# A gated mix of attention and feed-forward: the Q scratch holds whole 51-row tiles, and the maximum over partitions moves from GpSimd to TensorE and VectorE

## The chip, the cores and the metric

The kernel runs on one core of a Trainium2 chip. The metric is the device time of one execution in microseconds (us), as the median of several runs. Beside the timed runs one execution was recorded by the hardware profiler; all rows below come from that one.

## The reference

A token block x (2048 x 512) goes through two branches that a gate mixes:

```python
g = sigmoid((x * gate_w).sum(-1, keepdims=True))
q = (x @ wq).reshape(B, S, H, Dh).transpose(0, 2, 1, 3)    # 32 heads of 16
k, v = x @ wk, x @ wv                                      # one head, shared
p = softmax(einsum("bhqd,bkd->bhqk", q, k) * Dh ** -0.5)
a = einsum("bhqk,bkd->bhqd", p, v)....reshape(B, S, H * Dh) @ wo
b = (gelu(x @ w_gate) * (x @ w_up)) @ w_down               # width 1376
return g * a + (1 - g) * b
```

## The kernel before

**Precision.** Every operand is split into a rounded high part and the remainder (`split`, L105 and L106), and a product is made of three TensorE passes. For the scores this is packed into one matmul: the 51 rows (`QK`) of a Q tile are 32 rows of Q (high part and remainder, 16 each), 16 rows of the high part once more (together 48, `KR`), and three rows of a shift. The tile `kp` holds the matching rows of K, and in its last row the number that the shift subtracts before the exponential. A Q tile `Q[u]` has two such groups of 51 partitions (from partition 0 and from partition 64), and two heads in each group, so a unit `u` covers four heads and 512 tokens. There are 32 units (4 token groups of 8 units).

**Prologue.** The loop over token groups runs in the order 1, 2, 3, 0. For each group TensorE projects K and V (`pk`) and then Q in four blocks of 128 columns (`pq`, through the PSUM buffers of `ps_s`, three of them). `post_q` (L176 to L182) takes a block out of PSUM: ScalarE copies the high part into `q2`, VectorE takes the absolute maximum into `qmx` and subtracts for the remainder, and SyncE stores `q2` into the DRAM scratch `scr[tg, b]`, 32 rows for 8 heads. `q2` has three buffers, so the copy of a block waits until the store three blocks earlier has landed. GpSimd writes the shift rows of all heads into a second scratch `shs` (L149), with 0, 0 and 1.

In the last group (token group 0) more work is laid in: a weight fetch `fetch_w(2)` on SyncE ahead of the group's stores, `split_w(0)` and `split_w(1)` on VectorE and GpSimd, `post_v`, and behind the third block `load_q(0)` and `load_q(1)`, which read the first two Q tiles back. `load_q` issues six DMAs for a unit: two of 32 rows, two of 16 rows that read the high part a second time (`load_qk`, L235 and L236), and two of 3 rows out of `shs` (L245). SyncE's queue works in the order of the program, and a DMA that has to wait holds up all that stand behind it.

**Bound and branch.** Then the largest |q| times the largest |k| bounds all scores. VectorE reduces `qmx` and `kmx` to one number per partition (L272, L273), GpSimd reduces over the partitions (`partition_all_reduce` into `mma`, L274), VectorE makes the product `cb`, the `flag` whether it is too large, and `row`, the shift, which goes into the last row of both groups of `kp` by two DMAs (L425). `fill(2)` (L426) issues the gate and the up projection of the first feed-forward chunk. Every engine loads the flag into a register and branches (L431, L432): if the flag is set, a long block computes exact maxima. With these inputs it is skipped, and each engine jumps over it.

**Main loop.** For each unit and each of 16 key blocks TensorE makes scores (`s`, L487), ScalarE their exponential (`p`, L490), TensorE the product with V (`acc`, L557), interleaved by the list `ORDER` with pieces of the feed-forward branch (`fill`): the gate `g`, the up projection `u` and the down projection `dn` of a chunk, by `chain_mm` (L299). The first scores come behind the gate of the second chunk. Q tiles have two buffers; unit `u + 1` is loaded at the third key block of unit `u`, on the same SyncE queue as the weight chunks (`st`, L196).

Of the kernel before, what the change touches and what calls it, by code (L numbers as in the profile page):

```python
# [19 lines left out]
P = 128  # L20
S = 2048
D = 512
H = 32
DH = 16
F = 1376
TG = 512
NTG = S // TG
# [3 lines left out]
NB = 4  # L31
KR = 48
QK = 51
# [12 lines left out]
def mix_kernel(ctx, tc, xT, wq, wkv, wo, wf, out):  # L46
    nc = tc.nc
    cp = ctx.enter_context(tc.tile_pool(name="cp", bufs=1))
    dr = ctx.enter_context(tc.tile_pool(name="dr", bufs=1, space=DRAM))
    ps_s = ctx.enter_context(tc.tile_pool(name="ps_s", bufs=3, space=PSUM))  # L50
# [1 line left out]
    ps_f = ctx.enter_context(tc.tile_pool(name="ps_f", bufs=1, space=PSUM))  # L52
    ctx.enter_context(tc.manual_schedule())

    scr = dr.tile([NTG, NB, 32, 8, TG], F32, name="scr")
    shs = dr.tile([NTG, 3, H, TG], F32, name="shs")

    kp = cp.tile([P, S], F32R, name="kp")
    v1 = cp.tile([P, NKC, 32], F32, name="v1")
# [6 lines left out]
    qmx = cp.tile([P, NTG * NB], F32, name="qmx")  # L66
    kmx = cp.tile([P, NTG], F32, name="kmx")
    mm2 = cp.tile([P, 2], F32, name="mm2")
    mma = cp.tile([P, 2], F32, name="mma")
    cb = cp.tile([P, 1], F32, name="cb")  # L70
    sh = cp.tile([P, 1], F32, name="sh")
    flag = cp.tile([P, 1], I32, name="flag")
    woh = cp.tile([P, NB, D], F32R, name="woh")
    wol = cp.tile([P, NB, D], F32R, name="wol")

# [34 lines left out]
    ident = cp.tile([P, P], F32, name="ident")  # L110
# [34 lines left out]
    zz = woh[0:H]  # L145
    nc.gpsimd.memset(zz.bitcast(F32), 0.0)
    nc.gpsimd.memset(zz[:, 2].bitcast(F32), 1.0)
    for g in range(NTG):
        nc.gpsimd.dma_start(shs[g].rearrange("r h q -> h r q"), zz[:, 0:3].bitcast(F32))  # L149

    def passes(ps, lh, ll, rh, rl, n, first=True, last=True):
        seq = [(i, a, b) for i in range(n) for a, b in ((lh, rh), (ll, rh), (lh, rl))]
        for q, (i, a, b) in enumerate(seq):
            nc.tensor.matmul(ps, a(i), b(i), start=(first and q == 0), stop=(last and q == len(seq) - 1),
                             skip_group_check=True)

    def post_k(tg, pk):
        sl = slice(tg * TG, (tg + 1) * TG)
        for r in (0, 64):
            nc.scalar.copy(kp[r : r + KR, sl], pk[0:KR])  # L160
        nc.scalar.copy(vt[32 * tg : 32 * tg + 32], pk[64:96])
        nc.vector.tensor_reduce(kmx[0:KR, tg : tg + 1], pk[0:KR], axis=AX, op=ALU.max, apply_absolute_value=True)
        for r in (32, 96):
            nc.vector.tensor_sub(kp[r : r + 16, sl], pk[32:48], kp[r : r + 16, sl])
# [8 lines left out]
            nc.vector.tensor_copy(v2[:, i::4, 16:32], t[:, :, 0:16])  # L173
            nc.vector.tensor_copy(zt[:, i::4], t[:, :, 16:17].rearrange("p g r -> p (g r)"))

    def post_q(tg, b, pq):  # L176
        q2 = p2.tile([P, 2, TG], F32R, tag="q2", name=f"q2{tg}_{b}", bufs=3)
        i = tg * NB + b
        nc.scalar.copy(q2[:, 0], pq)
        nc.vector.tensor_reduce(qmx[:, i : i + 1], pq, axis=AX, op=ALU.max, apply_absolute_value=True)  # L180
        nc.vector.tensor_sub(q2[:, 1], pq, q2[:, 0])
        nc.sync.dma_start(scr[tg, b].rearrange("(t d) h q -> (d h) t q", t=2), q2.bitcast(F32))  # L182

    chunks = [(tg, f) for tg in range(NTG) for f in range(NF)]
    W = {}
# [7 lines left out]
    def fetch_w(n):  # L193
        if n < len(chunks):
            stage[n] = cp.tile([P, 3, D], F32, tag="st", name=f"st{n}", bufs=2)
            nc.sync.dma_start(stage[n], wf[chunks[n][1]].rearrange("p (t d) -> p t d", t=3))  # L196
# [30 lines left out]

    Q = {}

    def load_qk(t, u):  # L230
        g, ub = divmod(u, 8)
        b, a = divmod(ub, 2)
        for j in range(2):
            hs = slice(4 * a + j, 4 * a + 4, 2)
            nc.sync.dma_start(t[64 * j : 64 * j + 32].bitcast(F32), scr[g, b, 0:32, hs])  # L235
            nc.sync.dma_start(t[64 * j + 32 : 64 * j + KR].bitcast(F32), scr[g, b, 0:16, hs])  # L236

    def load_q(u, shift=True, data=True):
        g, ub = divmod(u, 8)
        if data:  # L240
            Q[u] = cp.tile([P, 2, TG], F32R, tag="Q", name=f"Q{u}", bufs=2)
            load_qk(Q[u], u)
        if shift:
            for j in range(2):
                nc.sync.dma_start(Q[u][64 * j + KR : 64 * j + QK].bitcast(F32), shs[g, :, 4 * ub + j : 4 * ub + 4 : 2])  # L245

    fetch_w(0)
    fetch_w(1)
    for ti, tg in enumerate(order):
        if ti == NTG - 1:  # L250
            fetch_w(2)
        xh, xl = xs[tg]
        pk = ps_a.tile([P, TG], F32, tag="pa", name=f"pk{tg}")
        passes(pk, lambda c: wkh[:, c], lambda c: wkl[:, c], lambda c: xh[:, c], lambda c: xl[:, c], NC)
        post_k(tg, pk)
        for b in range(NB):
            pq = ps_s.tile([P, 2 * TG], F32, tag="s", name=f"pq{tg}_{b}")[:, 0:TG]
            bs = slice(b * P, (b + 1) * P)
            passes(pq, lambda c: wqh[:, c, bs], lambda c: wql[:, c, bs], lambda c: xh[:, c], lambda c: xl[:, c], NC)
            if ti + 1 < NTG:  # L260
                split_x(order[ti + 1], b)
            post_q(tg, b, pq)
            if ti == NTG - 1 and b == 0:
                split_w(0)
            if ti == NTG - 1 and b == 1:
                post_v()
            if ti == NTG - 1 and b == 2:
                load_q(0)
                load_q(1)
                split_w(1)  # L270

    nc.vector.tensor_reduce(mm2[:, 0:1], qmx, axis=AX, op=ALU.max)  # L272
    nc.vector.tensor_reduce(mm2[:, 1:2], kmx, axis=AX, op=ALU.max)  # L273
    nc.gpsimd.partition_all_reduce(mma, mm2, P, bass_isa.ReduceOp.max)  # L274
    nc.scalar.activation(gt, zt, AF.Tanh, bias=0.0, scale=0.5)
    nc.vector.tensor_scalar(gc, gt, -0.5, 0.5, op0=ALU.mult, op1=ALU.add)
    nc.vector.tensor_scalar(gt, gt, 0.5, 0.5, op0=ALU.mult, op1=ALU.add)
# [131 lines left out]
    def fill(k=1):  # L409
        for _ in range(k):  # L410
            next(filler, None)
# [4 lines left out]
                for fn in later.pop(s):  # L416
                    fn()

    nc.vector.tensor_mul(cb, mma[:, 0:1], mma[:, 1:2])
    nc.vector.tensor_scalar(flag, cb, BOUND / DH, None, op0=ALU.is_gt)  # L420
    nc.vector.tensor_scalar(sh, cb, -1.01 * DH, None, op0=ALU.mult)
    row = zz[0:1].rearrange("p a b -> p (a b)")
    nc.vector.tensor_scalar(row, row, 0.0, sh[0:1], op0=ALU.mult, op1=ALU.add)
    for r in (QK - 1, 64 + QK - 1):
        nc.sync.dma_start(kp[r : r + 1].bitcast(F32), row.bitcast(F32))  # L425
    fill(2)  # L426
    pro.close()
    mp = ctx.enter_context(tc.tile_pool(name="mp", bufs=1))
    base = now[0] + 1
# [2 lines left out]
    with tc.If(v > 0):  # L432
        with tc.tile_pool(name="gp", bufs=1) as gp:
            zr = gp.tile([1, S], F32, name="zr")
            nc.vector.memset(zr, 0.0)
            for r in (QK - 1, 64 + QK - 1):
                nc.sync.dma_start(kp[r : r + 1].bitcast(F32), zr)
            for g in range(NTG):
                mx = gp.tile([P, 4, H, 2], F32, tag="mx", name=f"mx{g}")
                for ub in range(8):  # L440
                    t = gp.tile([P, 2, TG], F32R, tag="gq", name=f"gq{g}_{ub}", bufs=2)
                    load_qk(t, 8 * g + ub)
# [22 lines left out]
                nc.sync.dma_start(shs[g].rearrange("r h q -> h r q"), nb.bitcast(F32))  # L465
            load_q(0, data=False)
            load_q(1, data=False)


    m2 = ctx.enter_context(tc.tile_pool(name="m2", bufs=1))  # L470
# [115 lines left out]
    g = NTG - 1  # L586
# [50 lines left out]
```

## Time and profile before

| | us |
|---|---|
| median of 3 runs | 1305.08 |
| lowest and highest | 1304.79, 1305.23 |
| the profiled execution | 1305.77 |
| its span, from the first to the last instruction | 1304.0 |
| TensorE busy (matmul) | 1282.3 |
| ScalarE busy | 1023.1 |
| VectorE busy | 545.2 |
| GpSimd busy | 208.8 |

The profile counts an engine as busy while it executes; matmuls are pipelined, and their ends are modelled. L12 is line 12 of the kernel file. A row of the timeline gives the start and the duration in us, engine, line, operation, output from inputs, the count, and in brackets the idle time before it and what ended that. SPq is SyncE's queue of DMA issues; a name with q at its end (PEldq, DVEq) is the sequencer of that engine. The DMA share is the mean busy share of the 16 DMA engines.

### The profile page before, as it was taken

The numbers are of one execution on the slowest core, as the hardware profiler recorded it, in microseconds if no ns is written. First come the engines' busy times: TensorE is split into PE (matmuls) and PEld (weight loads), VectorE is DVE, ScalarE is ACT, GpSimd is POOL, SyncE is SP. The second block draws the span as 40 slices with busy tenths as digits, with TensorE's granted clock in tenths as the row PEclk, the third lists the DMA queues.
The fourth block names the chain that finished last, engine by engine and source line by source line (L and its number), as shares of the span: only waits on it lengthen the run. The fifth ranks groups of instructions, "written<-read, shape, count | busy, mean of one in ns | idle before, by whom it ended". The sixth has DMA issues, their size and how long they took to land.

```text
span 1304.0 us, 20303 instructions
## 1 busy us (share of the span) xinstructions
PE 1282.3 (98%) x8178; PEld 648.0 (50%) x8178; DVE 545.2 (42%) x829; ACT 1023.1 (78%) x1118; POOL 208.8 (16%) x173
## 2 busy tenths in 40 slices
PE   9969999999999999999999999999999999999998
PEld 6844445444454444445444455454445444445444
DVE  6753352624443162633435144252526134344334
ACT  5338888888888788888888878888887788888884
POOL 3122121202120021121212012021122011202010
PEclk9979999999999999999999999999999999999999
DMA  8441011111110211111111021110211211011100
GB/s 307 143 142 52 30 35 62 37 62 49 59 38 1 70 62 38 62 37 47 41 46 38 30 78 38 62 38 2 78 54 38 70 62 38 11 52 38 38 1 33
DMA packets 25204, 72.43 MB, mean 56 GB/s; under 512 B 3888, under 2 KB 3920, under 8 KB 25104
## 3 DMA queue, kind: packets, MB, share of 16 engines
q1 hardware_dynamic: 24704, 70.02, 16.0%
q8 instruction: 66, 1.08, 0.3%
q0 software_dynamic: 256, 0.79, 0.1%
q10 hardware_dynamic: 144, 0.26, 0.1%
q14 instruction: 34, 0.28, 0.1%
HBM read 57.67 MB, written 13.37 MB: 54 GB/s over the span
## 4 chain that ended last, share of the span: by engine, by line
PE 90%; ACT 2%; issue 1%; DVE 0%; ACTq 0%; DVEq 0%
PE acc L557 36%; PE s L487 23%; PE g L299 10%; PE u L299 10%; PE dn L299 8%; PE wo L299 3%; ACT p L490 2%; PE wos L299 1%; DVE acc L310 0%; PE wof L299 0%; DVE sq L362 0%; DVE sq L355 0%; DVE gs L384 0%; ACT sq L359 0%; ACTq L490 0%
## 5 line engine op out<-in xcount | busy, mean ns | idle before, releaser
L490 ACT ACTIVATE p<-s 128x1024 f32<-128x1024 f32 x1024 | 972.7, 1028 | 213.3 <-PE s L487 207.9
L557 PE MATMUL acc<-p,v 128*32 128x512 f32 x4096 | 479.2, 597 | 0.0
L487 PE MATMUL s<-Q,kp 51*128 51x512 f32 x2048 | 337.2, 429 | 4.5 <-ACT p L490 4.5
L487 PEld LDWEIGHTS s<-Q,kp 51*128 51x128 f32 x2048 | 165.0, 184 | 243.8 <-issue 160.2
L106 POOL TENSOR_TENSOR gl<-st,gh 128x512 fp32r<-128x512 f32 x88 | 122.8, 1415 | 994.8 <-DVE gh L105 783.1
L557 PEld LDWEIGHTS acc<-p,v 128*32 128x32 f32 x4096 | 113.5, 109 | 259.4 <-issue 253.1
L338 DVE SCALAR_TENSOR_TENSOR acc<-dn,gc,acc 128x512 f32<-128x512 f32 x48 | 35.7, 745 | 203.6 <-PE dn L299 203.6
L352 DVE COPY gs<-g 128x512 f32<-128x512 f32 x44 | 29.8, 677 | 174.3 <-PE g L299 174.3
L299 PE MATMUL g<-xh,gh 128*128 128x512 f32 x176 | 74.6, 424 | 11.8 <-DVE sq L355 10.9
L299 PE MATMUL dn<-dh,hh 128*128 128x512 f32 x176 | 75.9, 432 | 0.0
L299 PE MATMUL u<-xh,gh 128*128 128x512 f32 x176 | 73.7, 419 | 0.0
L299 PE MATMUL g<-xl,gh 128*128 128x512 f32 x176 | 69.8, 397 | 0.0
L299 PE MATMUL g<-xh,gl 128*128 128x512 f32 x176 | 69.6, 396 | 0.0
L299 PE MATMUL dn<-dl,hh 128*128 128x512 f32 x176 | 69.1, 392 | 0.0
L299 PE MATMUL u<-xl,gh 128*128 128x512 f32 x176 | 68.9, 392 | 0.0
L299 PE MATMUL dn<-dh,hl 128*128 128x512 f32 x176 | 68.7, 390 | 0.0
L299 PE MATMUL u<-xh,gl 128*128 128x512 f32 x176 | 68.6, 390 | 0.0
L105 DVE CAST dh<-st 128x512 fp32r<-128x512 f32 x44 | 65.4, 1486 | 0.0
L384 DVE SCALAR_TENSOR_TENSOR gs<-u,sq 128x512 f32<-128x512 f32 x44 | 30.5, 692 | 82.2 <-PE u L299 81.1
L523 DVE RECIPROCAL ntz<-nr 128x128 f32<-128x128 f32 (+1 forms) x62 | 56.5, 950 | 0.6
L106 POOL TENSOR_TENSOR dl<-st,dh 128x512 fp32r<-128x512 f32 x44 | 56.7, 1289 | 0.0
L362 DVE SCALAR_TENSOR_TENSOR sq<-sq,gs 128x512 f32<-128x512 f32 x44 | 30.6, 696 | 56.8 <-ACT sq L359 56.8
(111 smaller groups left out, 966.7 us busy)
## 6 DMA issues: line engine op xcount, KB each, us to landing
st<-wf SPq DMA_DIRECT2D x44, 768.0 KB
scr<-q SPq DMA_DIRECT2D x16, 512.0 KB
Q<-scr SPq DMA_DIRECT2D x64, 128.0 KB
Q<-scr SPq DMA_DIRECT2D x64, 64.0 KB
out<-acc SPq DMA_DIRECT2D x16, 256.0 KB
xr<-xT SPq DMA_DIRECT2D x6, 512.0 KB
xst<-xT SPq DMA_DIRECT2D x6, 512.0 KB
xr<-xT SPq DMA_DIRECT2D x4, 256.0 KB
```

Source lines behind the costliest of these rows:

```text
L105: eng_h.tensor_copy(hi, src)
L106: eng_l.tensor_sub(lo, src, hi)
L299: nc.tensor.matmul(ps, a, b, start=(first and q == 0), stop=(last and q == len(terms) - 1), skip_group_check=True)
L338: nc.vector.scalar_tensor_tensor(o, ps, w, o, op0=ALU.mult, op1=ALU.add)
L352: nc.vector.tensor_copy(gs, ps)
L362: nc.vector.scalar_tensor_tensor(sq, sq, 1.0, gs, op0=ALU.add, op1=ALU.mult)
L384: nc.vector.scalar_tensor_tensor(gs, ps, 0.5, sq, op0=ALU.mult, op1=ALU.mult)
L487: nc.tensor.matmul(ps[:, j * TG : (j + 1) * TG], kp[rs, kc * P : (kc + 1) * P], Q[u][rs, pr], start=True, stop=True)
L490: nc.scalar.activation(p, ps, AF.Exp, bias=0.0, scale=SCALE)
L523: nc.vector.reciprocal(z[:, cs], r[:, cs])
L557: nc.tensor.matmul(accp[u][32 * j : 32 * j + 32], vt[:, kc], pb[s, j // 2][:, (j % 2) * TG : (j % 2 + 1) * TG], start=(kc == 0), stop=(kc ...
```

## The change

The scratch gets 51 rows for each group and block, so that a Q tile's rows lie there as they are needed. The store of a block becomes two DMAs: 32 rows as before, and the high part once more into rows 32 to 47. GpSimd writes the three shift rows of every block into rows 48 to 50, by 16 DMAs of 8 partitions instead of 4 of 32. `load_q` reads 51 rows at once: two DMAs for a unit. The first two loads stand behind all 16 blocks' stores instead of behind the third block of the last group.

In the last block the absolute maximum and the two reductions stand ahead of ScalarE's copy. The reduction over partitions becomes two TensorE transposes of one column each into one PSUM partition, and one VectorE maximum over 2 x 128 elements; `cb`, `sh` and `flag` are one element instead of 128 partitions. The two steps of `fill(2)` are taken apart: the gate stands ahead of the transposes, the up projection behind the two DMAs into `kp`.

```diff
-    scr = dr.tile([NTG, NB, 32, 8, TG], F32, name="scr")
-    shs = dr.tile([NTG, 3, H, TG], F32, name="shs")
+    scr = dr.tile([NTG, NB, QK, 8, TG], F32, name="scr")
...
     for g in range(NTG):
-        nc.gpsimd.dma_start(shs[g].rearrange("r h q -> h r q"), zz[:, 0:3].bitcast(F32))
+        for b in range(NB):
+            nc.gpsimd.dma_start(scr[g, b, KR:QK].rearrange("r h q -> h r q"), zz[0:8, 0:3].bitcast(F32))
...
+        def bound():
+            nc.vector.tensor_reduce(qmx[:, i : i + 1], pq, axis=AX, op=ALU.max, apply_absolute_value=True)
+
+        if last:
+            bound()
+            nc.vector.tensor_reduce(mm2[:, 0:1], qmx, axis=AX, op=ALU.max)
+            nc.vector.tensor_reduce(mm2[:, 1:2], kmx, axis=AX, op=ALU.max)
         nc.scalar.copy(q2[:, 0], pq)
-        nc.vector.tensor_reduce(qmx[:, i : i + 1], pq, axis=AX, op=ALU.max, apply_absolute_value=True)
+        if not last:
+            bound()
         nc.vector.tensor_sub(q2[:, 1], pq, q2[:, 0])
-        nc.sync.dma_start(scr[tg, b].rearrange("(t d) h q -> (d h) t q", t=2), q2.bitcast(F32))
+        nc.sync.dma_start(scr[tg, b, 0:32].rearrange("(t d) h q -> (d h) t q", t=2), q2.bitcast(F32))
+        nc.sync.dma_start(scr[tg, b, 32:KR].rearrange("d h q -> (d h) q"), q2[:, 0].bitcast(F32))
...
-    def load_qk(t, u):
+    def load_q(u, t=None, rows=slice(0, QK)):
...
         for j in range(2):
-            hs = slice(4 * a + j, 4 * a + 4, 2)
-            nc.sync.dma_start(t[64 * j : 64 * j + 32].bitcast(F32), scr[g, b, 0:32, hs])
-            nc.sync.dma_start(t[64 * j + 32 : 64 * j + KR].bitcast(F32), scr[g, b, 0:16, hs])
...
+            dst = (Q[u] if t is None else t)[64 * j + rows.start : 64 * j + rows.stop]
+            nc.sync.dma_start(dst.bitcast(F32), scr[g, b, rows, 4 * a + j : 4 * a + 4 : 2])
...
             if ti == NTG - 1 and b == 2:
-                load_q(0)
-                load_q(1)
                 split_w(1)
 
-    nc.vector.tensor_reduce(mm2[:, 0:1], qmx, axis=AX, op=ALU.max)
-    nc.vector.tensor_reduce(mm2[:, 1:2], kmx, axis=AX, op=ALU.max)
-    nc.gpsimd.partition_all_reduce(mma, mm2, P, bass_isa.ReduceOp.max)
+    load_q(0)
+    load_q(1)
...
-    nc.vector.tensor_mul(cb, mma[:, 0:1], mma[:, 1:2])
+    fill()
+    pm = ps_s.tile([P, 2 * TG], F32, tag="s", name="pm")[0:1, 0 : 2 * P]
+    for j in range(2):
+        nc.tensor.transpose(pm[:, j * P : (j + 1) * P], mm2[:, j : j + 1], ident)
+    nc.vector.tensor_reduce(mm1, pm.rearrange("o (j p) -> o j p", j=2), axis=AX, op=ALU.max)
+    nc.vector.tensor_mul(cb, mm1[:, 0:1], mm1[:, 1:2])
...
-    fill(2)
+    fill()
```

The skipped block behind the flag is changed to match.

More of the change, by code (lines that the diff above doesn't have):

```diff
@@ L68, in mix_kernel @@
     mm2 = cp.tile([P, 2], F32, name="mm2")
[L69 to L72, printed above, removed]
+    mm1 = cp.tile([1, 2], F32, name="mm1")
+    cb = cp.tile([1, 1], F32, name="cb")
+    sh = cp.tile([1, 1], F32, name="sh")
+    flag = cp.tile([1, 1], I32, name="flag")
     woh = cp.tile([P, NB, D], F32R, name="woh")
@@ L174, in post_v, with post_q @@
             nc.vector.tensor_copy(zt[:, i::4], t[:, :, 16:17].rearrange("p g r -> p (g r)"))
-    def post_q(tg, b, pq):
+    def post_q(tg, b, pq, last):
         q2 = p2.tile([P, 2, TG], F32R, tag="q2", name=f"q2{tg}_{b}", bufs=3)
         i = tg * NB + b
+        def bound():
[4 more added lines that the diff above has]
+            nc.vector.tensor_reduce(mm2[:, 1:2], kmx, axis=AX, op=ALU.max)
         nc.scalar.copy(q2[:, 0], pq)
-        nc.vector.tensor_reduce(qmx[:, i : i + 1], pq, axis=AX, op=ALU.max, apply_absolute_value=True)
+        if not last:
+            bound()
         nc.vector.tensor_sub(q2[:, 1], pq, q2[:, 0])
-        nc.sync.dma_start(scr[tg, b].rearrange("(t d) h q -> (d h) t q", t=2), q2.bitcast(F32))
+        nc.sync.dma_start(scr[tg, b, 0:32].rearrange("(t d) h q -> (d h) t q", t=2), q2.bitcast(F32))
+        nc.sync.dma_start(scr[tg, b, 32:KR].rearrange("d h q -> (d h) q"), q2[:, 0].bitcast(F32))
     chunks = [(tg, f) for tg in range(NTG) for f in range(NF)]
@@ L228, in mix_kernel @@
     Q = {}
-    def load_qk(t, u):
+    def load_q(u, t=None, rows=slice(0, QK)):
         g, ub = divmod(u, 8)
         b, a = divmod(ub, 2)
+        if t is None and u not in Q:
+            Q[u] = cp.tile([P, 2, TG], F32R, tag="Q", name=f"Q{u}", bufs=2)
         for j in range(2):
-            hs = slice(4 * a + j, 4 * a + 4, 2)
-            nc.sync.dma_start(t[64 * j : 64 * j + 32].bitcast(F32), scr[g, b, 0:32, hs])
-            nc.sync.dma_start(t[64 * j + 32 : 64 * j + KR].bitcast(F32), scr[g, b, 0:16, hs])
[L238 to L245, printed above, removed]
+            dst = (Q[u] if t is None else t)[64 * j + rows.start : 64 * j + rows.stop]
+            nc.sync.dma_start(dst.bitcast(F32), scr[g, b, rows, 4 * a + j : 4 * a + 4 : 2])
     fetch_w(0)
@@ L261, in mix_kernel @@
                 split_x(order[ti + 1], b)
-            post_q(tg, b, pq)
+            post_q(tg, b, pq, ti == NTG - 1 and b == NB - 1)
             if ti == NTG - 1 and b == 0:
@@ L441, in mix_kernel @@
                     t = gp.tile([P, 2, TG], F32R, tag="gq", name=f"gq{g}_{ub}", bufs=2)
-                    load_qk(t, 8 * g + ub)
+                    load_q(8 * g + ub, t, slice(0, KR))
                     for i in range(4):
@@ L464, in mix_kernel @@
                 nc.vector.tensor_sub(nb[:, 1], nm, nb[:, 0])
-                nc.sync.dma_start(shs[g].rearrange("r h q -> h r q"), nb.bitcast(F32))
-            load_q(0, data=False)
-            load_q(1, data=False)
+                for b in range(NB):
+                    nc.sync.dma_start(scr[g, b, KR:QK].rearrange("r h q -> h r q"), nb[8 * b : 8 * b + 8].bitcast(F32))
+            for u in range(2):
+                load_q(u, None, slice(KR, QK))
     m2 = ctx.enter_context(tc.tile_pool(name="m2", bufs=1))
```

## The prediction

> **What bounds the kernel now.** I read the span and the shares of the chain of waits first, then the chain at the start of the run, where the change lies.
>
> ```profile
> span 1304.0 us, 20303 instructions
> ...
> PE 90%; ACT 2%; issue 1%; DVE 0%; ACTq 0%; DVEq 0%
> ```
>
> TensorE carries 90% of the chain, and the change leaves its main loop alone. Time can move only where TensorE stands still: between the projections and the main loop. The timeline by engine shows that stretch (start, duration, instruction, idle time before it and what ended it): first TensorE, then ScalarE, then SyncE's queue, then VectorE.
>
> ```profile
> 68.05 0.39 PE L299 MATMUL u<-xh,gl 128*128 128x512 f32 x1
> 79.29 0.77 PE L299 MATMUL g<-xh,gh 128*128 128x512 f32 x1 [10.86 <-DVE sq L355]
> ...
> 68.20 0.59 ACT L179 CAST q<-pq 128x512 fp32r<-128x512 f32 x1 [7.26 <-DMA scr<-q]
> ...
> 61.51 0.35 SPq L196 DMA_DIRECT2D st<-wf  x1
> 61.95 2.51 SPq L182 DMA_DIRECT2D scr<-q  x3
> ```
>
> ```profile
> 68.82 0.69 DVE L180 TENSOR_REDUCE qmx<-pq 128x1 f32<-128x512 f32 x1 [3.91 <-ACT q L179]
> 69.43 0.68 DVE L181 TENSOR_TENSOR q<-pq,q 128x512 fp32r<-128x512 f32 x1
> 70.02 0.16 DVE L272 TENSOR_REDUCE mm<-qmx 128x1 f32<-128x16 f32 x1
> 70.10 0.15 DVE L273 TENSOR_REDUCE mm<-kmx 128x1 f32<-128x4 f32 x1
> 70.16 0.17 DVE L276 TENSOR_SCALAR gc<-gt 128x16 f32<-128x16 f32 x1
> 70.36 0.17 DVE L277 TENSOR_SCALAR gt<-gt 128x16 f32<-128x16 f32 x1
> 73.72 0.16 DVE L419 TENSOR_TENSOR cb<-mma 128x1 f32<-128x1 f32 x1 [3.19 <-POOL mma L274]
> 73.92 0.15 DVE L420 TENSOR_SCALAR flag<-cb 128x1 int32<-128x1 f32 x1
> 73.99 0.14 DVE L421 TENSOR_SCALAR sh<-cb 128x1 f32<-128x1 f32 x1
> 74.17 1.27 DVE L423 TENSOR_SCALAR woh<-woh,sh 1x2048 fp32r<-1x2048 f32 x1
> 75.37 0.67 DVE L352 COPY gs<-g 128x512 f32<-128x512 f32 x1
> ```
>
> The order of events: the last Q block's copy waits for its buffer until 68.20, that is for the store of the block three earlier, which left late because it stood behind a weight fetch (61.51). Then come the maximum, the GpSimd reduction (3.19 us of waiting) and the flag at 74.07. Every engine reads the flag and branches. TensorE's own branch:
>
> ```profile
> L432 PEldq COMPARE_BRANCH  x1: 3666/3666/3666, 75.3 to 75.3; - x1
> ```
>
> So TensorE starts 5.22 us after the flag (79.29 less 74.07); the releaser named in its row is a neighbour in time, the branch is the cause. From there the chain of waits runs:
>
> ```profile
> 79.29 5.46 PE g L299 x12
> 84.75 0.50 PE s L487 x2
> ...
> 90.48 3.02 PE g L299 x12
> ```
>
> The first scores start at 84.75, the second chunk's gate at 90.48; from there TensorE is the bound. The windows (length, busy time of five engines, clock, DMA share, GB/s):
>
> ```profile
> 66.00:70.00 4.00, 2.43 (x11) 1.69 (x9) 1.18 (x2) 0.70 (x2) 1.30 (x2) 1.00 1.04 401
> ...
> 71.00:72.00 1.00, 0.00 (x0) 0.00 (x0) 0.00 (x0) 0.00 (x0) 0.00 (x0) 0.55 0.90 225
> 84.00:85.00 1.00, 1.00 (x4) 0.35 (x5) 0.21 (x1) 0.00 (x0) 0.00 (x0) 0.62 1.01 422
> ```
>
> The DMA engines are full at 66 to 70 and move 401 GB/s, 25.1 GB/s each. TensorE's clock halves 2.7 us after its last matmul and comes back at about 84.8, 5.5 us after it restarts. That is why this first gate takes 5.46 us and the next 3.02.
>
> **The flag's path.** The bytes of each Q store rise from 512 to 768 KiB, so the store that the last copy waits for lands 262,144 B / 401 GB/s = 0.65 us later: 68.85 for 68.20. SyncE's extra issues hide behind the data. The maximum and the two reductions now come ahead of the copy, in VectorE's 3.91 us of idle time: nothing. After the copy VectorE does the subtraction (69.47), gc and gt (70.06 and 70.26, spaced as in the rows), then the gate's copy, which used to follow the row and now stands in front: 0.67, to 71.1. The two transposes have long been done, since TensorE is idle after 68.44. The new maximum reads 256 elements of one partition: between 0.16 (16 elements) and 0.69 (512), I take 0.35. Then cb and the flag in 0.4, so the flag stands at 71.85 instead of 74.07: 2.2 us gained. TensorE restarts at 77.1 and ends the gate at 82.5.
>
> **The loads' path.** Q0 and Q1 (four DMAs) now stand behind the last store and ahead of the two kp rows, and the first scores need Q0 and the kp rows. After 68.85 the queue holds three stores of 786,432 B: 5.9 us at 401 GB/s, to 74.7. SyncE has issued everything by then (the subtraction ends at 70.15, then eight issues at some 0.4 to 0.6 us). Then come four loads of 51 rows x 2 heads x 2,048 B = 208,896 B. On how many DMA engines? The DMA view gives the size classes and the issues, first and last of 14 groups (295 issues):
>
> ```profile
> DMA packets 25204, 72.43 MB, mean 56 GB/s; under 512 B 3888, under 2 KB 3920, under 8 KB 25104
> ...
> st<-wf SPq DMA_DIRECT2D x44, 768.0 KB
> ...
> Q<-shs SPq DMA_DIRECT2D x64, 12.0 KB
> ...
> kp<-woh SPq DMA_DIRECT2D x2, 8.0 KB
> ```
>
> No transfer has rows under 512 B, so the 3888 small packets are the completions. 64 loads of three rows and 231 others: 231 x 16 + 64 x 3 = 3888 exactly. So the 3-row loads ran on three engines, all others, whose row counts divide by 16, on sixteen. Every split in this trace is into equal shares, and 51 = 3 x 17 goes in equal shares onto three of sixteen engines at most. I take three. The Trainium skill says this outright (DMA: Bandwidth & Descriptors, section Why a DMA increments its semaphore by 16 and not by 1: the largest number up to 16 that divides the slowest dimension of both sides, always the lowest-numbered engines); the trace's count agrees for three rows, and no run here shows 51 yet.
>
> On three engines a load takes 208,896 B / 75.2 GB/s = 2.78 us. Nothing in the trace tells one engine from another; loads of one shape I take to use the same three, one behind the other: 11.1 us, to 85.85. On another three each time they would overlap, which is the first rival's side. A kp row has sixteen pieces, one on each engine, so it stands behind these loads too: it lands at about 85.9, and the first scores start there instead of 84.75: 1.15 us later, though the flag is 2.2 us earlier. The flag's gain of 2.25 is eaten by 3.4 us of new waiting at the first scores, and TensorE works in order, so the up projection and all that follows wait with them.
>
> That wait leaves TensorE idle from 82.5 to 85.9, 3.4 us, longer than the 2.7 after which the clock halved in this trace. If it halves, six score matmuls and twelve of the up projection stand between the first scores and the second gate. Twelve took 5.46 us at half clock and 3.02 at full, which with the last one's end left out is about 0.44 and 0.24 us each. With the clock back after 5.5 us, 12.5 of the eighteen run at half, the other 5.5 take 1.3 us, and with the product on VectorE and its hand-overs (0.9) the second gate starts 7.7 us after the first scores instead of 5.73: 2.0 us. If the clock stays up it is nothing, if all eighteen run at half 3.1. I take 2.0, since the idle time is past the 2.7. The skill (TensorE: Matmul & The Clock Gate, What's actually happening) lets the clock fall after an idle window of about 3.4 us that runs free of the kernel; by that an idle time of 3.4 us may or may not cost, as the trace's 2.7 also leaves open.
>
> Sum: 1.15 + 2.0 = 3.15 us (in the 1.15 the flag's 2.25 is already taken off). The profiled execution took 1305.77 us, its span of 1304.0 and 1.8 around it; with 3.15 it would take 1308.9. It lies 0.7 above the median of 1305.08, so for the median the forecast is 1308.2.
>
> **What lies under cover.** In the first group the same wait for a store grows by 0.65:
>
> ```profile
> 25.12 0.59 ACT L179 CAST q<-pq 128x512 fp32r<-128x512 f32 x1 [5.00 <-DMA scr<-q]
> ...
> 30.84 0.68 DVE L181 TENSOR_TENSOR q<-pq,q 128x512 fp32r<-128x512 f32 x1
> ...
> 32.42 0.39 PE L154 MATMUL pq<-xh,wqh 128*128 128x512 f32 x1
> ...
> 57.40 2.83 POOL L106 TENSOR_TENSOR gl<-st,gh 128x512 fp32r<-128x512 f32 x2 [44.10 <-DVE gh L105]
> ```
>
> The subtraction that frees the score buffer for the matmul at 32.42 ends at 31.52, and then at 32.2: covered by 0.2 us; without cover it costs a few tenths. GpSimd issues 16 small DMAs instead of 4, in its 44.10 us of idle time: nothing. In the main loop each unit's loads fill three engines for 5.6 us, and the weight fetch behind them two at a time (1.57 MB, 3.9 us) waits for them; the tightest unit:
>
> ```profile
> 762.49 0.39 SPq L235 DMA_DIRECT2D Q<-scr  x1
> ...
> 777.97 0.76 DVE L105 CAST gh<-st 128x512 fp32r<-128x512 f32 x2
> ```
>
> The weights would land some 10 to 11 us after the Q issue and are used after 15.5: nothing. Four DMA issues fewer in each unit free SyncE, which nobody waits for.
>
> **The rivals.** *The loads spread (0.15).* If 51 rows go onto nearly all engines, or each load onto another three, the four loads take 2.1 us at 401 GB/s, the kp rows are there by 77.5, before the gate ends at 82.5, and the flag's gain stands: -2.25 us, 1302.8 (1302.2 to 1303.5). This is the other side: no loss. It decides when a load uses more than eight engines or so. For it: no row shows 51; against it: the completions. *Three engines, but the clock stays up (0.18).* +1.15 us, 1306.2. For it: 3.4 us is near the limit. *The main loop suffers too (0.07).* If the weights come later than 15.5 us after the Q issue, VectorE stands and TensorE follows in each of 31 units; 0.2 us each makes 6 us, 1314. Against it: 4 us of slack.
>
> **How the numbers follow.** The forecast has 0.60: 1308.2, its own range 1306.8 to 1309.8 (the landing of the kp rows is uncertain by 0.8 us, and I let the clock's part lie between 1.0 and 3.1). About 0.2%, 2.6 us, is what a measurement of this kernel can tell from no change, so the limit lies at 1307.7, just under the forecast: of its 0.60 I give 0.40 to slower and 0.20 to same. The full clock is same (0.18), the main loop slower (0.07), the spread loads half faster, half same (0.07, 0.08). That makes 0.07 faster, 0.46 same, 0.47 slower. The range 1302.3 to 1311.0 takes in the spread loads and leaves out the main loop's case.
>
> **What would show it.** Right: the DMA view counts 64 Q loads of 204 KB, and the small packets come to some 2288 (195 issues, of which these 64 leave three completions and 131 sixteen) and not to 3120; the flag at about 71.9; TensorE restarts near 77; then a gap before the first scores that ends with a DMA at about 86; a second dip of the clock behind it. Wrong: the first scores follow the gate at once, at about 82.5 (the loads spread), or VectorE waits for weights in the main loop.

## The result and the profile after

The changed kernel took 1315.15 us (median of 6 runs, 1313.40 to 1316.82), the kernel before 1304.79 (6 runs, 1303.74 to 1305.23). The ratio is 1.0080, with a 95% interval of 1.0067 to 1.0093: it is slower, and above 1311.0, the top of the forecast's range. The profiled execution of after took 1314.27 us. Its span is 8.5 us longer than that of before, and those 8.5 us are what the rows below account for. (The medians are 10.4 us apart; this execution lies low among the six of after, and the profiled one of before, 1305.77, lies above the six timed ones.)

The page of after: the span, the size classes of the DMA packets, the shares of the chain of waits, and the Q loads and stores.

```profile
span 1312.5 us, 20149 instructions
...
DMA packets 25970, 76.61 MB, mean 58 GB/s; under 512 B 2544, under 2 KB 2576, under 8 KB 25872
...
q0 software_dynamic: 768, 0.79, 0.5%
...
PE 90%; ACT 2%; issue 1%; DVE 0%; ACTq 0%
...
Q<-scr SPq DMA_DIRECT2D x64, 204.0 KB
```

The chain still has TensorE at 90%: the main loop did not change. The difference lies in the first 100 us. The timeline of after, with the rows that answer to those of before: the first group's fourth copy and the wait of TensorE that follows from it, the work on the last group's weights, the last copy, the new maximum, the flag, TensorE's restart and the first scores.

```profile
30.89 0.59 ACT L187 CAST q<-pq 128x512 fp32r<-128x512 f32 x1 [11.21 <-DMA scr<-q]
...
32.85 0.79 PE L154 MATMUL pq<-xh,wqh 128*128 128x512 f32 x1 [3.44 <-DVE q L190]
...
63.57 2.83 POOL L105 TENSOR_TENSOR gl<-st,gh 128x512 fp32r<-128x512 f32 x2 [39.08 <-DVE gh L104]
...
74.99 0.59 ACT L187 CAST q<-pq 128x512 fp32r<-128x512 f32 x1 [7.88 <-DMA scr<-q]
...
77.10 0.40 DVE L422 TENSOR_REDUCE mm<-pm 1x2 f32<-1x256 f32 x1
...
77.72 0.14 DVE L424 TENSOR_SCALAR flag<-cb 1x1 int32<-1x1 f32 x1
...
84.34 0.77 PE L298 MATMUL g<-xh,gh 128*128 128x512 f32 x1 [9.28 <-PEq L436]
92.71 1.05 PE L492 MATMUL s<-Q,kp 51*128 51x512 f32 x6 [2.91 <-SPq L436]
```

The copy that the prediction had under cover starts at 30.89 instead of 25.12. From there everything in the prologue is late: GpSimd's row at 57.40 of before now stands at 63.57, 6.17 us later. The chain of waits then shows the start of the main loop:

```profile
92.71 1.05 PE s L492 x6
93.76 4.52 PE u L298 x12
...
99.18 2.95 PE g L298 x12
```

The second chunk's gate starts at 99.18, 8.70 us later than the 90.48 of before; the span is 8.5 us longer. So all but 0.2 us of the loss is there by that point. In steps, from rows of the two profiles:

| Step | predicted | measured |
|---|---|---|
| everything up to the last group (GpSimd's row, 57.40 to 63.57) | 0 | +6.17 |
| the last copy behind larger stores (68.20 to 74.99, less 6.17) | +0.65 | +0.62 |
| from the copy to the flag (5.87 us, now 2.87) | -2.87 | -3.00 |
| from the flag to TensorE's restart (5.22, now 6.48) | 0 | +1.26 |
| from the restart to the first scores (5.46, now 8.37) | +3.37 | +2.91 |
| from the first scores to the second gate (5.73, now 6.47) | +2.0 | +0.74 |
| sum | +3.15 | +8.70 |

Why the first group's copy is late shows in the windows from 21 to 27 us. Columns: length, busy time of TensorE, its weight load, VectorE, ScalarE and GpSimd, granted clock, DMA share, GB/s. First before, then after:

```profile
21.00:27.00 6.00, 6.00 (x29) 4.95 (x28) 1.98 (x4) 1.85 (x4) 0.00 (x0) 1.00 0.96 375
```

```profile
21.00:27.00 6.00, 6.00 (x29) 4.95 (x28) 0.27 (x1) 0.00 (x0) 2.04 (x4) 1.00 1.05 216
```

The DMA engines are just as full, but they move 216 GB/s instead of 375. GpSimd's timeline in after shows the issues of its 16 small DMAs (the first and the last rows of six), spread from 11.07 to 24.50 us; in before the four issues ended at 13.30. Their packets run to 32.9 us. SyncE's timeline shows two store issues of some 4 us each:

```profile
11.07 4.66 POOL L149 DMA_DIRECT2D scr<-woh  x8 [0.31 <-POOL woh L146]
...
23.37 1.13 POOL L149 DMA_DIRECT2D scr<-woh  x2 [1.31 <-DMA scr<-woh]
...
19.66 4.14 SPq L191 DMA_DIRECT2D scr<-q  x1
23.84 3.94 SPq L192 DMA_DIRECT2D scr<-q  x1
```

The software queue q0 carries the same 0.79 MB as before, but its share of the engines' time went from 0.1% to 0.5%. Its line in before:

```profile
q0 software_dynamic: 256, 0.79, 0.1%
```

In the packet records its 4096-byte packets take 159 to 172 ns in before, all of them; in after half still take 159, but 5% take over 1.2 us and the longest 2.0 us.

### The profile page after: what moved, and what is told of

It reads as the page before. It is cut to its first block, busy times and chain, and to the rows that moved or that the text cites. A ratio compares the mean times of both kernels' runs of the same rounds, so it can differ in the third digit from the quotient of the medians.

```text
span 1312.5 us, 20149 instructions
## 1 busy us (share of the span) xinstructions
PE 1286.6 (98%) x8180; PEld 651.0 (50%) x8180; DVE 544.9 (42%) x830; ACT 1023.2 (78%) x1118; POOL 214.8 (16%) x184
## 2 busy tenths in 40 slices
DMA packets 25970, 76.61 MB, mean 58 GB/s; under 512 B 2544, under 2 KB 2576, under 8 KB 25872
## 4 chain that ended last, share of the span: by engine, by line
PE 90%; ACT 2%; issue 1%; DVE 0%; ACTq 0%
PE acc L562 36%; PE s L492 23%; PE u L298 10%; PE g L298 9%; PE dn L298 8%; PE wo L298 3%; ACT p L495 2%; PE wos L298 1%; DVE acc L309 0%; PE wof L298 0%; ACTq L495 0%
```

## The experiments

**1. GpSimd's DMAs alone, on the kernel before.** Theory A: the 16 small DMAs are the loss. Rival B: it is the larger stores. This kernel has the small stores of before.

```diff
-        nc.gpsimd.dma_start(shs[g].rearrange("r h q -> h r q"), zz[:, 0:3].bitcast(F32))
+        for b in range(NB):
+            nc.gpsimd.dma_start(shs[g, :, 8 * b : 8 * b + 8].rearrange("r h q -> h r q"), zz[0:8, 0:3].bitcast(F32))
```

> The kernel before, with one edit: GpSimd writes the shift rows by 16 DMAs of 8 partitions, all from the same 8 source partitions, instead of 4 of 32. Bytes and everything else are as before. In the changed kernel TensorE loses 6.2 us ahead of the last token group, because the copy that waits for a Q store starts at 30.89 us instead of 25.12, and 768 GpSimd packets lie between 15 and 33 us. Theory A (the 16 small GpSimd transfers hold the DMA engines, and SyncE's Q stores wait behind them): the copy moves to about 30 us here too, TensorE waits some 2.5 us in the second token group and its clock halves, 1308 to 1311 us. Rival B (the doubled store bytes are the cause, not the GpSimd DMAs): the copy stays at 25 us and the time at 1305.

1309.58 us against 1304.75, ratio 1.0034 (1.0020 to 1.0049). Its timeline and its window:

```profile
31.80 0.59 ACT L180 CAST q<-pq 128x512 fp32r<-128x512 f32 x1 [11.69 <-DMA scr<-q]
```

```profile
21.00:27.00 6.00, 6.00 (x28) 4.95 (x28) 0.71 (x2) 0.00 (x0) 1.96 (x4) 1.00 1.03 262
```

The copy is as late as in after and the rate is down to 262 GB/s (375 in before), with stores of the old size. B falls as the cause of the early loss.

**2. The same 16 DMAs, each from partitions of its own.** A1: what counts is that all of them read the same eight partitions. A2: it is their number or their shape. The only edit against the first experiment:

```diff
-            ... zz[0:8, 0:3].bitcast(F32))
+            ... zz[8 * b : 8 * b + 8, 0:3].bitcast(F32))
```

> As the run with 16 GpSimd DMAs in the kernel before, but each block's DMA reads its own 8 of 32 source partitions instead of all reading the same 8. Theory A1 (many engines reading the same 8 partitions is what makes these transfers slow): the GpSimd packets take their normal 159 ns again, time 1305. Theory A2 (the number of DMAs or their 8-way split is what makes them slow): as the other run, 1308 to 1311 us. Rival B (doubled store bytes): 1305 in both.

1305.07 us, ratio 1.0002 (0.9992 to 1.0011): the loss is gone. Its timeline:

```profile
24.94 0.59 ACT L180 CAST q<-pq 128x512 fp32r<-128x512 f32 x1 [4.76 <-DMA scr<-q]
```

Sixteen DMAs cost nothing that shows; sixteen that read the same eight partitions cost 4.8 us. (Here four of them, one for each token group, share a set of eight, where all sixteen did before.) A1 holds.

**3. The changed kernel with the source spread.** All of `woh` gets the 0, 0, 1 rows, and each of the 16 DMAs reads eight partitions of its own out of 128.

```diff
-            ... zz[0:8, 0:3].bitcast(F32))
+            ... woh[32 * b + 8 * g : 32 * b + 8 * g + 8, 0:3].bitcast(F32))
```

> The changed kernel with one edit: the zeros and ones are laid into all 128 partitions, and each of the 16 GpSimd DMAs reads its own 8 partitions. Theory A1 (common source partitions): the 6.2 us of the prologue come back but for some tenths, the flag, the branch and the first scores are as in the changed kernel less 6.2, so about 1309 us. Theory A2 (number or shape of the DMAs) and rival B (bytes of the stores): no change, 1315.

1308.53 us (1307.76 to 1310.49), ratio 1.0029 (1.0017 to 1.0042): 6.6 us of the 10.4 are gone. Its timeline:

```profile
26.71 0.59 ACT L187 CAST q<-pq 128x512 fp32r<-128x512 f32 x1 [6.35 <-DMA scr<-q]
...
33.17 0.50 PE L154 MATMUL pq<-xh,wqh 128*128 128x512 f32 x1 [0.35 <-DVE q L190]
...
87.50 1.74 PE L492 MATMUL s<-Q,kp 51*128 51x512 f32 x6 [2.99 <-SPq L436]
```

Where TensorE waited 3.44 us in after it now waits 0.35, and the wait ahead of the first scores is left as it was (2.99 us). The copy is still 1.6 us later than in before, and the larger stores are what is left to explain it: they were not wholly under cover. What remains is near the forecast's 1308.2; how far that agreement is luck is told under the rivals below.

**4. The changed kernel with Q loads of 48 and 3 rows.** Theory C: the wait at the first scores comes from 51 rows running on three DMA engines. Rival D: it comes from the loads' place behind all stores. Here each load is two, of 48 rows (a multiple of 16) and of 3.

```diff
-            dst = (Q[u] if t is None else t)[64 * j + rows.start : 64 * j + rows.stop]
-            nc.sync.dma_start(dst.bitcast(F32), scr[g, b, rows, 4 * a + j : 4 * a + 4 : 2])
+            for lo, hi in ((0, KR), (KR, QK)):
+                lo, hi = max(lo, rows.start), min(hi, rows.stop)
+                if lo < hi:
+                    ...
```

> The changed kernel with one edit: a Q tile is loaded by 48 rows and 3 rows instead of 51 at once, so four DMAs for a unit. Theory C (a 51-row load runs on three DMA engines, and the first scores wait for the four loads there): the Q loads are over within some 3 us, the first scores follow the gate at about 90 us instead of 92.7, no idle time ends with SyncE there, about 1312 us. Rival D (the first scores wait for the branch of SyncE itself, whatever the loads do): first scores at 92 to 93 us, 1315. In both the 6.2 us lost in the prologue stay.

1311.85 us, ratio 1.0058 (1.0041 to 1.0075): 3.3 us better than after. Its timeline:

```profile
83.42 0.76 PE L301 MATMUL g<-xh,gh 128*128 128x512 f32 x1 [9.28 <-PEq L439]
...
88.55 0.96 PE L495 MATMUL s<-Q,kp 51*128 51x512 f32 x6
```

The first scores now follow the gate with no idle time ahead of them. C holds, D falls: same place in the queue, no wait. (Of the 4.16 us by which the first scores are earlier than in after, 0.92 were there at TensorE's restart.)

**5. Both repairs together.** The edits of experiments 3 and 4.

> The changed kernel with both repairs: GpSimd's small DMAs read from all partitions in turn (theory A) and each Q tile loads as 48 and 3 rows, which divide by 16 and by 3 (theory C). If the two losses are separate and are the whole loss, this is 1308.5 (the spread source alone) less 3.3 (what the 48 rows gained by themselves), about 1305.2; if the flag's gain of 2.25 us comes through in full, 1302.8. Theory D (the first scores are late because the loads stand behind all stores, whatever their shape) has a wait of TensorE at the first scores left and 1307 or more.

1305.64 us (10 runs, 1303.77 to 1308.30), ratio 1.0007 (0.9997 to 1.0016). One by one the repairs brought 6.6 and 3.3 us, together 9.5: they add up to within 0.4 us, as separate losses do. But the flag's gain does not show. The rows for that stand behind experiment 7.

**6. Only one unit's 51-row loads ahead of the kp rows** (source spread, `load_q(1)` issued behind the branch).

```diff
     load_q(0)
-    load_q(1)
...
+    load_q(1)    # behind the branch
```

> The changed kernel with the spread source, and the second unit's Q loads issued behind the branch, so that only two 51-row loads stand ahead of the kp rows. Theory C' (four loads in a row on three engines make the wait; each takes 2.8 us): the first scores follow the gate 5.6 us less late, that is at once, at about 84.6, and the time is 1305.2 to 1306 against 1308.5 with the spread source alone. Rival (the 51 rows or the place behind all stores as such): 1308, with the wait at the first scores left.

1305.67 us, ratio 1.0008 (0.9998 to 1.0018): 2.9 us better than experiment 3, although the loads have 51 rows as before. Its timeline:

```profile
77.34 0.77 PE L297 MATMUL g<-xh,gh 128*128 128x512 f32 x1 [8.85 <-PEq L435]
...
82.73 1.11 PE L491 MATMUL s<-Q,kp 51*128 51x512 f32 x6
```

There is no wait at the first scores: from the restart to them it is 5.39 us, where it was 8.11 in experiment 3. (TensorE also restarts 2.05 us earlier here. Of that, 1.4 us come from the last copy, which is nothing that this edit touches.) So what cost time was not a 51-row load as such, but four of them in a row on the same three engines.

**7. The flag's path alone, on the kernel before.** Early maximum, two transposes, one VectorE maximum, the two fill steps taken apart; scratch, stores, loads and GpSimd's DMAs as before.

> The kernel before with the flag's path of the change alone: the last block's maximum and the reductions ahead of the copy, two transposes and one VectorE maximum for the GpSimd reduction, the two fill steps taken apart; scratch, stores, loads and GpSimd's small DMAs as before. Theory E (the new reduction is a gain by itself that the other parts bury): the flag some 2.3 us earlier (71.8 for 74.07), TensorE's gate and the first scores as much earlier, 1302.0 to 1302.8. Rival F (the flag does not set the first scores: something else, the kp rows or the loads on SyncE, is late next): 1304.5 to 1305.5 with a wait at the first scores.

1302.59 us (10 runs, 1301.39 to 1304.69), ratio 0.9987 (0.9977 to 0.9996): faster, by 2.1 us. Its timeline, and the row of TensorE's branch:

```profile
68.54 0.59 ACT L187 CAST q<-pq 128x512 fp32r<-128x512 f32 x1 [7.13 <-DMA scr<-q]
...
71.27 0.14 DVE L431 TENSOR_SCALAR flag<-cb 1x1 int32<-1x1 f32 x1
...
76.33 0.77 PE L305 MATMUL g<-xh,gh 128*128 128x512 f32 x1 [6.97 <-PEq L443]
```

```profile
L443 PEldq COMPARE_BRANCH  x1: 3966/3966/3966, 72.0 to 72.0; - x1
```

The flag stands at 71.41, 2.66 us earlier than in before, and TensorE restarts 2.96 us earlier. E holds: this part of the change is a gain by itself. F falls: the first scores (81.03) follow the gate with no wait. The repaired kernel of experiment 5 has the same part, and in its profiled execution loses it so:

```profile
69.52 0.59 ACT L187 CAST q<-pq 128x512 fp32r<-128x512 f32 x1 [7.81 <-DMA scr<-q]
...
79.47 0.77 PE L301 MATMUL g<-xh,gh 128*128 128x512 f32 x1 [9.82 <-PEq L439]
```

```profile
L439 PEldq COMPARE_BRANCH  x1: 5532/5532/5532, 73.6 to 73.6; - x1
```

Its last copy is 0.98 us later than in experiment 7 (most of that from the larger stores, as far as one execution of each can say), its branch starts another 0.6 us later after the flag, and the branch takes 1.57 us longer. TensorE restarts 3.14 us later. (The medians are 3.05 us apart and the two profiled executions 5.4; what the clock adds is in the last section.)

**8. The flag's path, and the weight fetch moved behind the Q loads.** In before, `fetch_w(2)` stands ahead of the last group's stores, and the last copy waits for one of those stores. It is one transfer of 768 KB: the expectation's 1.57 MB and 3.9 us are those of two, and one is 2.0 us at 401 GB/s. Nor is it its bytes alone that hold the stores up. SyncE's waits in before (50 to 80 us) show that the fetch itself waits until GpSimd has done with the staging buffer that it is to fill (61.49), and the stores wait behind it, though the first one's data were ready at 56.98:

```profile
SPq L196 <- POOL dl L106: 9.8, 1, 9.8
```

```diff
-        if ti == NTG - 1:
-            fetch_w(2)
...
                 load_q(0)
                 load_q(1)
+                fetch_w(2)
```

> As the kernel before with the flag's path of the change, and also the weight fetch of the third chunk moved from ahead of the last group's stores to behind the first two units' Q loads. Theory G (the last block's copy waits for a store that stands behind 1.57 MB of weights, 3.9 us at 401 GB/s): the last copy starts about 3.9 us earlier than 68.20, the flag with it, 1298 to 1299.5. Rival H (the stores themselves or TensorE's projections set the last copy, the fetch only fills a gap): 1302 to 1303, as with the flag's path alone.

1305.23 us, ratio 1.0000 (0.9990 to 1.0010): neither theory's time. Its timeline and its branch:

```profile
65.83 0.58 ACT L187 CAST q<-pq 128x512 fp32r<-128x512 f32 x1 [4.64 <-DVE qmx L181]
...
68.92 0.14 DVE L430 TENSOR_SCALAR flag<-cb 1x1 int32<-1x1 f32 x1
...
77.06 0.77 PE L304 MATMUL g<-xh,gh 128*128 128x512 f32 x1 [7.92 <-PEq L442]
```

```profile
L442 PEldq COMPARE_BRANCH  x1: 7052/7052/7052, 69.7 to 69.7; - x1
```

G was right up to the flag, though not in the size: the copy starts 2.71 us earlier than in experiment 7 (3.9 expected) and waits for a store no more, and the flag stands 2.35 us earlier. But TensorE's branch takes 7.05 us instead of 3.97, and the restart is 0.73 us later than without the move. The two profiled executions are 3.3 us apart; most of the rest lies in the first two gates, by the chains of waits of experiment 7 and of this one:

```profile
76.33 4.79 PE g L305 x12
...
87.93 3.02 PE g L305 x12
```

```profile
77.06 5.47 PE g L304 x12
...
89.35 4.60 PE g L304 x12
```

Twelve matmuls take longer there because more of them run at half clock (the last section comes back to this).

**9. The same fetch issued behind the branch.**

```diff
+    fetch_w(2)
     m2 = ctx.enter_context(tc.tile_pool(name="m2", bufs=1))
```

> The kernel before with the flag's path of the change, and the weight fetch of the third chunk issued behind the branch instead of ahead of the last group's stores. With the fetch between the Q loads and the branch, TensorE's branch took 7.05 us against 3.97 and the 2.35 us that the flag had gained were lost again. Theory J (the branch takes as long as it does because the block of instructions that it jumps to comes over the same DMA engines, behind the data queued there): with the fetch out of the way the flag stands at about 69.1, the branch takes 4 us or less, TensorE restarts at about 74 and the time is 1299.5 to 1301. Rival K (the branch ends at a time that something else sets, at about 77, whatever the flag does): the branch takes 7 us again, 1305.

1300.65 us (6 runs, 1299.81 to 1303.13) against 1305.11, ratio 0.9967 (0.9955 to 0.9979). It is faster than both kernels: 4.5 us below before. Its timeline and its branch:

```profile
68.76 0.14 DVE L429 TENSOR_SCALAR flag<-cb 1x1 int32<-1x1 f32 x1
...
74.04 0.76 PE L303 MATMUL g<-xh,gh 128*128 128x512 f32 x1 [5.04 <-DVE sq L359]
```

```profile
L441 PEldq COMPARE_BRANCH  x1: 4186/4186/4186, 69.5 to 69.5; - x1
```

The flag comes when it did in experiment 8, but the branch takes 4.19 us (J had 4 or less) and TensorE restarts 3.02 us earlier. The two kernels differ only in where SyncE issues the fetch, so moving the data out of the way shortened the branch: J holds, K falls. The packet records show the way: between a branch's start and its end the instruction queue q8 moves one packet of 16,384 bytes. It starts 1.1 us after the branch in before, 4.5 us after it in experiment 8 and 1.8 us in experiment 9. In each of the three the branch ends 1.5 us after the packet has landed.

The Trainium skill (Runtime: NRT & Kernel Launch, section Instruction fetch mechanics) says that a taken branch whose target is not in the window of two loaded pages of 16 KiB forces a DMA fetch of the target before execution goes on. The trace agrees in the size and the order. That the kernel's own data can hold this fetch up shows in the 7.05 and 4.19 us here; at which point of the DMA path it waits does not show.

**10. The changed kernel with all repairs and the late fetch.** The edits of experiments 3, 4 and 9.

> The changed kernel with the spread source and the loads of 48 and 3 rows, and the same weight fetch issued behind the branch. The stores of the last group no longer stand behind 1.57 MB: the last copy starts 3 to 4 us earlier than 69.5. Theory J: the queue also empties earlier, but it still holds three stores of 768 KiB and eight loads when the branch asks for its instructions, so the branch keeps 4.5 to 5.5 us; TensorE restarts 2 to 4 us earlier than 79.5, and the time is 1302 to 1303.5 against 1305.6. Rival K: no gain, 1305 to 1306.

1303.93 us (11 runs, 1301.73 to 1306.29), ratio 0.9992 (0.9983 to 1.0001): 0.4 us above J's range and 1.7 us better than experiment 5. Its timeline and its branch:

```profile
75.40 0.77 PE L299 MATMUL g<-xh,gh 128*128 128x512 f32 x1 [6.20 <-PEq L437]
```

```profile
L437 PEldq COMPARE_BRANCH  x1: 4972/4972/4972, 70.1 to 70.1; - x1
```

The branch took 4.97 us, inside J's 4.5 to 5.5, and TensorE restarts 4.07 us earlier than in experiment 5 (2 to 4 expected; the 1.57 MB is again that of two fetches). It restarts 1.36 us later than in experiment 9. The 51-row scratch can be had without a loss, but in no form run here does it bring a gain over the old one.

## Why the prediction was wrong

**The step that failed is "under cover: nothing" for GpSimd's 16 DMAs.** The prediction laid them into GpSimd's 44.10 us of idle time and stopped there. It counted the issues on an idle engine. It did not follow their transfers onto the 16 DMA engines, which SyncE's stores fill at that time, and it did not ask what `zz[0:8]` means for sixteen transfers together. That step gives +6.17 us of the 8.70, and experiments 1 to 3 show it. The prediction had quoted the covered wait in the first group itself (25.12) and knew how little cover there was: 0.9 us, of which 0.65 us of larger stores left 0.2. Where it put 0.65, 5.8 came. That was enough to reach TensorE by a shorter way than the one that it had followed: the matmul that waits (32.85) is the one that takes over the score buffer of the late block itself. In before it had 2.7 us to spare (the buffer was free at 27.03, the matmul started at 29.70).

**How the 5.8 us became 6.17.** TensorE's wait is 3.44 us, and while it lasts the clock falls. At half clock a matmul started every 0.43 us (32.85 and on) instead of every 0.23 us, until about 39. The wait put TensorE back by 3.6 us and the clock by 3.0; the profiled execution of after had begun its first block 0.45 us earlier than that of before (13.63 for 14.08), which leaves the 6.17 within a few hundredths.

**The last copy: right,** as far as one execution can say: +0.62 for +0.65, and +0.66 in experiment 3. **The flag's path: right, and slightly better.** The maximum over 256 elements took 0.40 us for an estimated 0.35. Experiment 7 shows the path as a gain alone.

**The restart after the flag: an unseen term.** The prediction kept the 5.22 us of before. In after it was 6.48, since the branch took 4.93 us instead of 3.67:

```profile
L436 SPq EVENT_SEMAPHORE  x8: 17/17/17, 88.0 to 92.6; - x8
...
L436 PEldq COMPARE_BRANCH  x1: 4932/4932/4932, 79.1 to 79.1; - x1
```

The prediction named the branch as the cause of the 5.22 us, but took its length as fixed. It depends on what is queued on the DMA engines when it is taken (experiments 8 and 9), and the change had just put stores and loads there. With the old stores and loads the branch took 3.47 to 3.99 us (before and experiments 1, 2 and 7), with the new ones 4.57 to 5.53 (after and experiments 3, 4, 5 and 6).

**Three engines: right.** Of the 2544 small packets 512 belong to GpSimd's queue (each of its 16 DMAs leaves 32), and the other 2032 are 115 x 16 + 64 x 3: each 51-row load ran on three engines, as the Trainium skill's rule (DMA: Bandwidth & Descriptors, section Why a DMA increments its semaphore by 16 and not by 1) has it. The predicted 2288 missed only that, with sixteen for each of GpSimd's. In the records the four loads take some 11.5 us (11.1 predicted), and the wait was 2.91 us for 3.4. The kp rows did land last, as predicted: in the packet records of after they are 32 packets of 512 bytes, of which 26 ended by 86.09 and the other six at 91.57 to 91.70, with the last Q packet at 91.64. In experiment 4 all 32 had ended by 83.56. The row of the wait names another releaser, SyncE's hand-over at the branch, the last of whose eight semaphore instructions starts at 92.6, 0.9 us after the last kp packet. Whether that hand-over waited for the kp rows or for Q1, which the first scores do not use, is not separated: experiment 6 takes Q1 out of both ways.

**The clock: right that it dips; how long it dips was not to be had from the figures that the prediction used.** The windows of after around the two dips (clock, DMA share and GB/s in the last three columns):

```profile
80.00:81.00 1.00, 0.00 (x0) 0.00 (x0) 0.00 (x0) 0.00 (x0) 0.00 (x0) 0.51 0.31 66
...
90.00:91.00 1.00, 0.00 (x0) 0.00 (x0) 0.97 (x2) 0.00 (x0) 0.00 (x0) 0.87 0.21 80
93.00:94.00 1.00, 1.00 (x7) 0.64 (x6) 1.00 (x1) 0.62 (x1) 1.00 (x2) 0.84 0.49 74
97.00:98.00 1.00, 1.00 (x6) 0.72 (x4) 0.48 (x1) 0.00 (x0) 0.00 (x0) 0.95 0.59 242
```

A mean of 0.87 in a window of 1 us that switches between 0.5 and 1 puts the edge at 90.26; the four edges are at 80.02, 90.26, 93.68 and 97.10. They lie 10.24, 3.42 and 3.42 us apart: whole multiples of 3.41. The prediction took 5.5 us of half clock, the time that the restart had needed in before, and from it 2.0 us; the dip was 3.42 us long. It made the up projection 1.6 us longer (4.52 us in the chain of after), but only 0.74 us of it reached the second gate, since in before TensorE had stood 0.95 us ahead of that gate, waiting for VectorE, and in after it did not. The prediction had added that hand-over on top of the matmuls, and had counted eighteen of these where six more scores stand behind the up projection (88.57 in before). The Trainium skill (TensorE: Matmul & The Clock Gate, What's actually happening) has a window of 3413 ns that runs free of the kernel. The edges agree. Read that way, instead of "2.7 us after the last matmul, 5.5 after the restart", the dip is a whole number of windows; it does not say how many. In the profiled execution of experiment 3 the same dip lasted two (87.38 to 94.22, from windows read in the same way) and cost 2.17 us, close to the 2.0 predicted.

**The main loop: right.** The loss is 8.70 us at the second gate and 8.5 at the end.

**The rivals.** The loads did not spread, and the main loop did not suffer. The forecast's own case came in for the loads, and with the one foreign cause taken away (experiment 3) the time is 1308.53. That agreement is partly luck. In after, the unseen 1.26 us at the branch and the 1.26 us too much for the clock cancel. The profiled execution of experiment 3 took 1310.49, the longest of its six. It has 0.89 us ahead of the last group and 1.55 at the branch that the sum did not have, and 0.72 less than predicted from the restart to the first scores (2.65 for 3.37).

## What to carry to other kernels

An issue that is free on an idle engine is not free: follow its bytes to the DMA engines, ask who fills these at that moment, and do not let a group of DMAs all read the same few partitions (four to a set cost nothing here, sixteen cost 4.8 us). Keep the row count of a load that stands ahead of a deadline a multiple of 16 (48 rows left no wait here, 51 left 2.9 us), or keep such loads few in a row. Ahead of a branch on a register, keep the DMA queues short: a transfer of 768 KB queued just ahead made TensorE's branch 7.05 us long, and 4.19 when it was issued behind. A weight fetch moved from ahead of the stores to behind the branch, with the shorter flag path, made the fastest version here.

## What the hardware showed that was not expected

Small GpSimd DMAs that read the same eight partitions slow the whole core's DMA: 216 to 262 GB/s instead of 375, at full engine share. Why the shared source does that (a port, a memory bank) no run here separates; that the sharing does it, experiments 1 and 2 show. A branch of TensorE took from 3.47 to 7.05 us by what was queued on the DMA engines when it was taken.

The executions of the repaired versions spread more than those of before, and the spread goes with the mean granted clock, which was taken for each timed execution. The ten of experiment 5 fall into five from 1303.77 to 1304.58, with a clock of 0.996 or 0.997, and five from 1306.69 to 1308.30, with 0.993 to 0.995; experiment 6 divides in the same way, with five up to 1304.98 and five from 1306.35. One dip of 3.41 us at half clock takes 0.0013 off the mean over 1305 us. In the profiled execution of experiment 5, the longest of its ten, a gate of twelve matmuls took 4.52 us at half clock; in that of experiment 7 the same gate took 3.02, although TensorE had stood idle for 2 us ahead of it in both.

This bears on experiment 8. Eight of its ten executions have a clock of 0.995 and two 0.997; in experiment 7 it was four and six. Among those at 0.997 the medians are 1302.62 and 1301.87, which are 0.75 us apart, close to the 0.73 us of the restart; most of the other 1.9 us between the two medians goes with how many executions had the lower clock (among those at 0.995 the two are 1.1 us apart). What stays open is why one execution gets the dip and the next does not. A free-running clock window that catches a short idle time in one and not in the other would do this, but no run was made to show it.
